# Linear attention and two expert MLPs on one core: a state tile without zero blocks, one masking per unit, other PSUM tiles and another start for the first sums of x

## The chip, the cores and the metric

The kernel runs on one core of a Trainium2 chip. The metric is the device time of one execution in microseconds; less is better. The kernel before takes 1306.77 us (median of three runs, 1305.92 to 1308.89).

The core has five engines with a queue each: PE (TensorE, matrix products into PSUM), DVE (VectorE), ACT (ScalarE), POOL (GpSimd) and SP (SyncE, which issues most DMAs). An engine runs its queue in order and waits on semaphores for the others.

## The reference

Three stages, cut to what is computed:

```python
# attention: state per batch and head, one step per token
state = alpha[:, :, t, :, None] * state + einsum('bhd,bhde->...', k[:, :, t], v[:, :, t])
y[:, :, t] = einsum('bhd,bhde->bhe', q[:, :, t], state)      # B=4, H=8, S=768, D=48
x = y as [3072, 384]
# first MLP
h = x @ w_in                                                  # 384 -> 2048
x = elu(h) @ w_out                                            # 2048 -> 384
# second: four experts, weighted by normalised probabilities
out = sum over e of p[:, e:e+1] * (relu(x @ w1[e]) @ w2[e])   # 384 -> 1024 -> 384
```

## The kernel before

**Attention** runs in chunks of 128 tokens: 6 chunks x 4 batches make 24 units. Heads lie in pairs, one at partitions 0 to 47, the other at 64 to 111. A unit has these steps (`unit_steps`, L333):

- `prep0` to `prep2` (L174 to L208): running products P of alpha (a scan on DVE), 1/P by logarithm and exponential on ACT, then k/P and q*P on DVE.
- `scores` (L210): eight matmuls of 48 rows, keys times queries, into two one-bank tiles (one for each j); DVE multiplies each by the causal mask (L224) into sm.
- `ktrans` (L230): four transposes of the keys into a third bank; ACT copies them to kn.
- `yout_t` (L257): four matmuls of the old state against the queries (L265; the stationary side is 112 columns wide: two heads of 48 with 16 unused columns between, zeros off the diagonal) and eight of values against masked scores (L272) into one bank; ACT copies the sum to yt (L277) and sends it to memory, from where SP loads it back as xr in the layout of the MLP. Units of the first chunk use `yout` instead.
- `state` (L287): eight matmuls of keys by values (L295), then DVE adds the old state and multiplies by P of the last token, once for each half of the partitions (L306, L308).
- `xtrans` (L312): high and low parts of the result in fp32r for the MLP.

The functions `abank` and `hbank` take PSUM banks in turn. Outside the warm-up the attention's banks are a0 and a1; the MLP's are h0 to h2, and t0 to t2 hold its result.

**First MLP.** 96 items: 6 blocks of 512 tokens, 16 slices of the hidden width each. `first(i)` is nine matmuls of 128 x 512 (L370: three parts of the width, each as high x high, high x low and low x high) and the elu: relu and exp on ACT (L381, L382), one DVE operation (L383), and the split of g into high (ACT, L330) and low (DVE, L331). `second(i-2)` is nine matmuls into t0 to t2 (L393). After a block's last item ACT copies t0 to t2 to x1raw (L850) and sends it out. The steps of a block's four units are spread over the items of the previous block. Here a list scheduler sets the order of the instructions on each engine from the order in which the code issues them; in the warm-up (the first chunk's units) and in the expert part the order on PE is the order of the code.

**First pair's sums.** `prep_x0` (L499) loads parts of the MLP's result, forms sums of them on POOL into the tile xs (L497), and splits these in fp32r: ACT rounds (L330), POOL subtracts (L331). xs lies in W1, a buffer that holds two slices of the MLP's weights until the last block has used them.

**Expert part.** 3 rounds of two chunks, 11 groups each. `layer1` makes 15 products of three matmuls (L650) into h banks, which DVE and POOL combine (L664, L666, L670), then relu on ACT and the low part on POOL (L628 to L630). `layer2` (L678) accumulates into six banks (m, d); the last matmul of an expert for (m, d) is followed by `gate` (L709): DVE multiplies the bank by the probabilities (L716, L719). Its matmuls of group i - 1 are dealt among the products of group i. In group 0 the last two `second()` stand there instead.

## Time and profile before

| what | us |
|---|---|
| median of three runs | 1306.77 |
| the profiled execution | 1309.81 |
| its span | 1308.1 |
| PE busy | 1258.4 (96%) |
| DVE busy | 890.6 (68%) |
| ACT busy | 582.7 (45%) |
| POOL busy | 518.4 (40%) |

The span runs from the first to the last instruction of the profiled execution; the execution's own time is 1.7 us longer. Busy time adds up the durations of an engine's instructions. PE is the only engine near the whole span. Of the chain of work that ended last, 65% of the span lies on PE, 11% each on DMA and DVE, 5% each on ACT and POOL. The mean granted clock of PE is 0.986 of full speed.

### The profile page before, as it was taken

How to read it: one execution, taken by the hardware profiler on the slowest of the kernel's cores; microseconds unless marked ns; L12 is line 12 of the kernel's file. 1: busy time of each engine (PE TensorE's matmuls, PEld its weight loads, DVE VectorE, ACT ScalarE, POOL GpSimd, SP SyncE). 2: the span in 40 equal slices, each digit the busy share in tenths (PEclk: the TensorE clock that was granted, in tenths of full speed). 3: DMA queues.
4: the chain of work that ended last, by engine and by line, in shares of the span. 5: the costliest groups of instructions: out<-in, count | busy, mean ns of one | idle time of the engine just before them, and what ended most of it. 6: DMA issues, size and time to landing. Idle time of an engine off the chain costs nothing.

```text
span 1308.1 us, 17463 instructions
## 1 busy us (share of the span) xinstructions
PE 1258.4 (96%) x6297; PEld 1014.6 (78%) x6297; DVE 890.6 (68%) x1546; ACT 582.7 (45%) x1076; POOL 518.4 (40%) x405
## 2 busy tenths in 40 slices
PE   8989999999999998889999999899999999999997
PEld 5676788778778787668888888788888878888886
DVE  9999988687777742366757666566667575767664
ACT  5666666566556564433434241333333233333241
POOL 0000000000000015348878474887966465447472
PEclk9999999999999999999999999999999999999999
DMA  6545366556666541425747348765645574525232
GB/s 246 195 164 178 109 221 239 189 203 214 242 223 216 188 147 73 173 93 194 258 159 278 114 161 335 256 243 183 255 167 199 185 296 166 195 97 204 102 109 75
DMA packets 71533, 246.67 MB, mean 189 GB/s; under 512 B 6680, under 2 KB 38264, under 8 KB 62096
## 3 DMA queue, kind: packets, MB, share of 16 engines
q1 hardware_dynamic: 68016, 236.84, 50.5%
q10 hardware_dynamic: 3424, 8.65, 1.9%
q8 instruction: 51, 0.84, 0.3%
q14 instruction: 42, 0.34, 0.1%
HBM read 182.11 MB, written 63.36 MB: 188 GB/s over the span
## 4 chain that ended last, share of the span: by engine, by line
PE 65%; DMA 11%; DVE 11%; ACT 5%; POOL 5%; issue 2%; SPq 1%; ACTq 0%; DVEq 0%; POOLq 0%
PE h L650 22%; PE t L700 13%; PE a L700 9%; PE t L393 7%; PE h L370 7%; DMA wraw<-in_we_dram 5%; PE h L700 4%; DMA x0d<-yt 2%; DMA raw<-in_att_dram 2%; DVE u L670 1%; DMA xr<-x0d 1%; DVE wh L331 1%; DVE P L181 1%; POOL xs L497 1%; DVE h L383 1%
## 5 line engine op out<-in xcount | busy, mean ns | idle before, releaser
L670 DVE TENSOR_TENSOR u<-h,u 128x512 f32<-128x512 f32 x258 | 177.5, 688 | 90.4 <-PE h L650 89.4
L393 PE MATMUL t<-g,w_W 128*128 128x512 f32 x864 | 226.1, 404 | 13.1 <-ACT g L330 12.5
L370 PE MATMUL h<-x,w_W 128*128 128x512 f32 x864 | 224.0, 402 | 3.7 <-ACT w_W L330 3.7
L650 PE MATMUL h<-xc_Q,wa 128*128 128x512 f32 x780 | 219.9, 391 | 3.3 <-DVE g L331 1.4
L630 POOL TENSOR_TENSOR g_W<-c,g_W 128x512 fp32r<-128x512 f32 x128 | 164.8, 1303 | 123.6 <-ACT c L629 105.5
L393 PEld LDWEIGHTS t<-g,w_W 128*128 128x128 f32 x864 | 162.5, 192 | 53.0 <-ACT g L330 14.6
L628 ACT ACTIVATE g_W<-c 128x512 fp32r<-128x512 f32 x128 | 80.0, 626 | 274.5 <-DVE c L670 159.9
L370 PEld LDWEIGHTS h<-x,w_W 128*128 128x128 f32 x864 | 162.8, 192 | 42.5 <-ACT w_W L330 5.1
L331 POOL TENSOR_TENSOR xc_X<-xr,xc_X 128x512 fp32r<-128x512 f32 x2 | 2.6, 1300 | 478.9 <-DMA xr<-x1d 478.7
L650 PEld LDWEIGHTS h<-xc_Q,wa 128*128 128x128 f32 x780 | 145.4, 188 | 37.4 <-DVE u L670 3.8
L700 PE MATMUL t<-g_W,wb 128*128 128x512 f32 x576 | 157.6, 389 | 0.0
L700 PEld LDWEIGHTS t<-g_W,wb 128*128 128x128 f32 x576 | 108.0, 188 | 22.6 <-POOL g_W L630 0.2
L629 ACT ACTIVATE c<-c 128x512 f32<-128x512 f32 x192 | 121.0, 632 | 7.4
L670 DVE TENSOR_TENSOR c<-u,h 128x512 f32<-128x512 f32 x123 | 84.1, 686 | 50.4 <-PE h L650 38.4
L664 DVE COPY u<-h 128x512 f32<-128x512 f32 x99 | 68.1, 690 | 68.3 <-PE h L650 68.0
L700 PE MATMUL a<-g_W,wb 128*128 128x512 f32 x384 | 112.0, 391 | 0.0
L630 POOL TENSOR_TENSOR g_X<-c,g_X 128x512 fp32r<-128x512 f32 x64 | 82.5, 1303 | 62.6 <-ACT c L629 52.0
L628 ACT ACTIVATE g_X<-c 128x512 fp32r<-128x512 f32 x64 | 40.0, 626 | 142.0 <-DVE c L670 78.5
L383 DVE SCALAR_TENSOR_TENSOR h<-e,h 128x512 f32<-128x512 f32 x96 | 66.5, 692 | 49.7 <-ACT e L382 49.2
L331 DVE TENSOR_TENSOR g<-h,g 128x512 fp32r<-128x512 f32 x96 | 66.0, 687 | 37.7 <-ACT g L330 36.7
L650 PE MATMUL h<-xc_W,wa 128*128 128x512 f32 x297 | 85.0, 395 | 4.9 <-DVE u L670 2.9
L700 PEld LDWEIGHTS a<-g_W,wb 128*128 128x128 f32 x384 | 72.4, 188 | 15.4 <-POOL g_W L630 0.3
(150 smaller groups left out, 1965.1 us busy)
## 6 DMA issues: line engine op xcount, KB each, us to landing
wa<-wad SPq DMA_DIRECT2D x33, 1536.0 KB, 6.6
wb<-wbd SPq DMA_DIRECT2D x30, 1536.0 KB, 6.5
raw<-in_att_dram SPq DMA_DIRECT2D x22, 960.0 KB, 5.1
wad<-wh SPq DMA_DIRECT2D x44, 384.0 KB, 2.8
wbd<-wh SPq DMA_DIRECT2D x43, 384.0 KB, 3.4
xcd<-xh SPq DMA_DIRECT2D x30, 512.0 KB, 3.7
wraw<-in_wm_dram SPq DMA_DIRECT2D x16, 768.0 KB, 4.3
wraw<-in_we_dram SPq DMA_DIRECT2D x20, 576.0 KB, 5.3
```

The costliest lines, as they stand in the source:

```text
L181: nc.vector.tensor_tensor_scan(P[:, a, :], raw[:, A0 + a * C:A0 + (a + 1) * C], self.plo.to_broadcast([128, C]), 1.0, ALU.mult, ALU.max,)
L331: (eng or nc.vector).tensor_tensor(out=lo, in0=src, in1=hi.bitcast(F32), op=ALU.subtract)
L370: nc.tensor.matmul(h[:, 0:n], w[:, wl, fi, k * 128:(k + 1) * 128], x[:, xl, k, n0:n0 + n], start=(k == 0 and i == 0), stop=(k == KD - 1 an ...
L383: nc.vector.scalar_tensor_tensor(out=h, in0=e, scalar=-1.0, in1=h, op0=ALU.add, op1=ALU.max)
L393: nc.tensor.matmul(self.xa[k][:, 0:n], w[:, wl, fi, DM + k * 128:DM + (k + 1) * 128], g[:, gl, 0:n], start=(f == 0 and i == 0), stop=(f == ...
L628: nc.scalar.activation(out=g[:, n, 0], in_=v, func=AF.Relu)
L629: nc.scalar.activation(out=v, in_=v, func=AF.Relu)
L630: nc.gpsimd.tensor_tensor(out=g[:, n, 1], in0=v, in1=g[:, n, 0].bitcast(F32), op=ALU.subtract)
L650: nc.tensor.matmul(b, w[:, wl], x[:, xl], start=(j == 0), stop=(j == 2))
L664: nc.vector.tensor_copy(out, b)
L670: (nc.vector if "b" in (a0, a1) or dst == "S5" else nc.gpsimd).tensor_tensor(out=out, in0=val(a0, b), in1=val(a1, b), op=ALU.add if op == ...
L700: nc.tensor.matmul(oa[m, d], wt[:, f, wl, d * 128:(d + 1) * 128], G[m][:, f, gl], start=first, stop=last)
```

## The change

- The state tile is 64 columns wide and without the zero blocks. The four matmuls of state against queries become eight of 48 rows and 64 columns (L271); the stationary side of `state`'s matmuls is 64 columns wide; DVE updates the state with one add and one multiplication over all 128 partitions.
- The eight score matmuls write one tile "a" of two banks, and one DVE operation masks all 1024 columns.
- `ktrans` follows the scores directly and takes an h bank. `state` follows `yout_t` directly in the order of the code, and `prep1` and `prep2` stand by themselves around the two.
- `yout_t` takes a new tile "a" and writes its first half; `state` writes the second half of the same tile (`abank`). In the warm-up the banks t0 to t2 serve.
- `layer2` accumulates m = 0 in the two halves of such a tile and h2, and m = 1 in t0 to t2.
- `prep_x0` begins at item b5 - 1 in place of b5 + 5 and spreads its 20 steps over 14 items in place of 9; xs lies in X0 (the MLP's input of the blocks with even number) in place of W1; the tiles xc and wa take other buffers accordingly, and xc tiles are taken as they are needed.
- The h banks stay three during group 0 of the expert part.

Lines after L114 shift by up to 6: L265 becomes L271, L272 L278, L277 L283, L295 L301, L330 L331, L650 L652, L700 L703, L716 L719, L719 L722, L850 L853. L370, L381 to L383 and L393 keep their numbers.

PE around one unit's state and output, kernel before (second chunk's first units; x is the MLP's input, sm the masked scores, st the state, kn the transposed keys):

```order
L235 MATMUL a_1597<-ident,raw 128x128 [waits DVE_49]
L235 MATMUL a_1597<-ident,raw 128x128 x3
L370 MATMUL h_1612<-x_1_689,w_W_640 128x512 x9
L265 MATMUL a_1629<-raw,st_150 112x128 [waits DVE_49]
L265 MATMUL a_1629<-raw,st_150 112x128 x3
L272 MATMUL a_1629<-sm,raw 48x128 x8
L393 MATMUL t_1504<-g,w_W_532 128x512 [waits Activation_49]
L393 MATMUL t_1504<-g,w_W_532 128x512 x2
L393 MATMUL t_1505<-g,w_W_532 128x512 x3
L393 MATMUL t_1506<-g,w_W_532 128x512 x3
L295 MATMUL a_1661<-raw,kn 48x48 [waits Activation_49]
L295 MATMUL a_1661<-raw,kn 48x48 x7
```

The same steps of a unit in the changed kernel, from the first() ahead of the state's product on:

```order
L370 MATMUL h_2445<-x_0_1490,w_W_636 128x512 [waits DVE_49]
L370 MATMUL h_2445<-x_0_1490,w_W_636 128x512 x8
L271 MATMUL a<-raw,st_150 64x128 [waits DVE_49]
L271 MATMUL a<-raw,st_150 64x128 x7
L278 MATMUL a<-sm,raw 48x128 x8
L393 MATMUL t_2309<-g,w_W_516 128x512 [waits Activation_49]
L393 MATMUL t_2309<-g,w_W_516 128x512 x2
L393 MATMUL t_2310<-g,w_W_516 128x512 x3
L301 MATMUL a<-raw,kn 64x48 [waits Activation_49]
L301 MATMUL a<-raw,kn 64x48 x7
L393 MATMUL t_2311<-g,w_W_516 128x512 x3
L370 MATMUL h_2512<-x_0_1490,w_W_734 128x512 [waits PE_49]
```

The transposes (L235) have gone up to the scores; the state's matmuls (now L301) stand six wide matmuls (L393) behind yout_t's last one (L278) where nine stood, write the same tile, and wait for ACT.

PE at the end of the first expert for the accumulators that come last, kernel before (t_5391 to t_5393 are t0 to t2):

```order
L700 MATMUL t_5391<-g_W_5749,wb 128x512 [waits Activation_49]
L700 MATMUL t_5391<-g_W_5749,wb 128x512 [waits Pool_49]
L700 MATMUL t_5391<-g_W_5749,wb 128x512
L650 MATMUL h_5863<-xc_Q_4864,wa 128x512 [waits DVE_49]
L650 MATMUL h_5863<-xc_Q_4864,wa 128x512 x2
L700 MATMUL t_5392<-g_W_5749,wb 128x512 x3
L650 MATMUL h_5878<-xc_Q_4864,wa 128x512 [waits DVE_49]
L650 MATMUL h_5878<-xc_Q_4864,wa 128x512 x2
L700 MATMUL t_5393<-g_W_5749,wb 128x512 x3
L700 MATMUL t_5391<-g_W_5749,wb 128x512
```

The same place in the changed kernel (a is the tile of two banks):

```order
L703 MATMUL a<-g_W_5704,wb 128x512
L652 MATMUL h_5845<-xc_Q_4933,wa 128x512 [waits DVE_49]
L652 MATMUL h_5845<-xc_Q_4933,wa 128x512 x2
L703 MATMUL a<-g_W_5704,wb 128x512 x2
L703 MATMUL a<-g_W_5704,wb 128x512 [waits DVE_49]
L652 MATMUL h_5860<-xc_W_5017,wa 128x512 x3
L703 MATMUL a<-g_W_5704,wb 128x512 x2
L703 MATMUL h_5351<-g_W_5704,wb 128x512
L652 MATMUL h_5869<-xc_W_5017,wa 128x512 x3
L703 MATMUL h_5351<-g_W_5704,wb 128x512 x2
```

Where the step from the first to the second accumulator stood without a wait (t_5391 to t_5392), the first matmul into the second half of a waits for DVE.

ACT at the end of the fifth block, kernel before (h_4643 and h_4686 are the last block's first two items, x1raw the copies of the fifth block's result):

```order
L381 ACTIVATE e<-h_4643 128x512 [waits PE_49]
L382 ACTIVATE e<-e 128x512 [waits Activation_49]
L330 CAST g<-h_4643 128x512 [waits DVE_49]
L381 ACTIVATE e<-h_4686 128x512 [waits PE_49]
L382 ACTIVATE e<-e 128x512 [waits Activation_49]
L850 COPY x1raw<-t_4033 128x512 [waits PE_49]
L850 COPY x1raw<-t_4034 128x512 [waits PE_49]
L330 CAST g<-h_4686 128x512 [waits DVE_49]
L850 COPY x1raw<-t_4035 128x512 [waits PE_49]
L851 DMA x1d_70<-x1raw 128x1536 [waits DMAHW1_49,Activation_49]
```

The same place in the changed kernel (h_4600 and h_4662 are the last block's first two items):

```order
L381 ACTIVATE e<-h_4600 128x512 [waits PE_49]
L331 CAST xc_Q_4776<-xs 128x512 [waits Pool_49]
L382 ACTIVATE e<-e 128x512 [waits Activation_49]
L331 CAST xc_Q_4776<-xs 128x512 [waits Pool_49]
L331 CAST xc_Q_4933<-xs 128x512 [waits Pool_49]
L331 CAST g<-h_4600 128x512 [waits DVE_49]
L331 CAST xc_Q_4933<-xs 128x512 [waits Pool_49]
L381 ACTIVATE e<-h_4662 128x512 [waits PE_49]
L853 COPY x1raw<-t_3986 128x512 [waits PE_49]
L382 ACTIVATE e<-e 128x512 [waits Activation_49]
L853 COPY x1raw<-t_3987 128x512 [waits PE_49]
L853 COPY x1raw<-t_3988 128x512 [waits PE_49]
```

The roundings of the sums xs, which all stood behind these copies, now stand in part ahead of them.

The diff, without the parts that only follow from it:

```diff
@@ -112,9 +112,14 @@
-    def abank(self):
-        self.an += 1
-        return self.bank(self.ab[self.an % len(self.ab)])
+    def abank(self, new=False):
+
+        if self.ab:
+            self.an += 1
+            return self.bank(self.ab[self.an % len(self.ab)])
+        if new:
+            self.a2 = self.ps.tile([128, 2, 512], F32, tag="a", name="a")
+        return self.a2[:, 0 if new else 1]
@@ -135,7 +140,7 @@
         for b in range(B):
-            s = self.ap.tile([128, NP, SW], F32, tag=f"st{b}", name=f"st{b}")
+            s = self.ap.tile([128, NP, 64], F32, tag=f"st{b}", name=f"st{b}")
             nc.vector.memset(s, 0.0)
@@ -211,26 +216,25 @@
         raw = self.raw[u]
-        ps = [self.abank(), self.abank()]
+        ps = self.ps.tile([128, 2, 512], F32, tag="a", name="a")
         for a in range(NP):
                 nc.tensor.matmul(
-                    ps[j][:, a * C:(a + 1) * C], raw[r, K0 + a * C:K0 + (a + 1) * C],
+                    ps[:, j, a * C:(a + 1) * C], raw[r, K0 + a * C:K0 + (a + 1) * C],
                     raw[r, Q0 + a * C:Q0 + (a + 1) * C], start=True, stop=True,
                 )
-        for j in range(2):
-            sm = self.ap.tile([128, NP, C], F32, tag="sm", name="sm", bufs=2)
-            nc.vector.tensor_tensor(
-                out=sm, in0=ps[j].rearrange("p (a t) -> p a t", a=NP),
-                in1=self.mask.unsqueeze(1).to_broadcast([128, NP, C]), op=ALU.mult,
-            )
-            self.sm[u, j] = sm
+        sm = self.ap.tile([128, 2 * NP, C], F32, tag="sm", name="sm")
+        nc.vector.tensor_tensor(
+            out=sm, in0=ps.rearrange("p j (a t) -> p (j a) t", a=NP),
+            in1=self.mask.unsqueeze(1).to_broadcast([128, 2 * NP, C]), op=ALU.mult,
+        )
+        self.sm[u] = sm
         raw = self.raw[u]
-        ps = self.abank()
+        ps = self.hbank()
         for a in range(NP):
@@ -260,18 +264,20 @@
         raw = self.raw[u]
-        ps = self.abank()
+        ps = self.abank(True)
         for a in range(NP):
-            nc.tensor.matmul(
-                ps[0:SW, a * C:(a + 1) * C], self.st[b][:, a, :], raw[:, Q0 + a * C:Q0 + (a + 1) * C],
-                start=(a == 0), stop=False, skip_group_check=True,
-            )
+            for j in range(2):
+                r = slice(64 * j, 64 * j + D)
+                nc.tensor.matmul(
+                    ps[64 * j:64 * j + 64, a * C:(a + 1) * C], self.st[b][r, a, :], raw[r, Q0 + a * C:Q0 + (a + 1) * C],
+                    start=(a == 0), stop=False, skip_group_check=True,
+                )
         for a in range(NP):
                     ps[64 * j:64 * j + D, a * C:(a + 1) * C], raw[:, V0 + h * D:V0 + (h + 1) * D],
-                    self.sm[u, j][:, a, :], start=False, stop=True, skip_group_check=True,
+                    self.sm[u][:, j * NP + a, :], start=False, stop=True, skip_group_check=True,
                 )
@@ -282,32 +288,27 @@
         self.y[u] = x
-        del self.sm[u, 0], self.sm[u, 1]
+        del self.sm[u]
         raw, kn, pc = self.raw.pop(u), self.kn.pop(u), self.P.pop(u)[:, :, C - 1:C]
-        st = self.st[b]
+        st = self.st[b][:, :, 0:D]
         ps = self.abank().rearrange("p (a e) -> p a e", a=NP)
             nc.tensor.matmul(
-                ps[64 * j:64 * j + D, h // 2, 0:D],
-                kn[:, (h // 2) * C + 64 * j:(h // 2) * C + 64 * j + D],
+                ps[64 * j:64 * j + 64, h // 2, 0:D],
+                kn[:, (h // 2) * C + 64 * j:(h // 2) * C + 64 * j + 64],
                 raw[:, V0 + h * D:V0 + (h + 1) * D], start=True, stop=True, skip_group_check=True,
             )
+        src = ps[:, :, 0:D]
         if c:
             tmp = self.ap.tile([128, NP, D], F32, tag="tmp", name="tmp")
-        for j in range(2):
-            r, e = slice(64 * j, 64 * j + D), slice(64 * j, 64 * j + D)
-            src = ps[r, :, 0:D]
-            if c:
-                nc.vector.tensor_tensor(out=tmp[r], in0=src, in1=st[r, :, e], op=ALU.add)
-                src = tmp[r]
-            nc.vector.tensor_tensor(
-                out=st[r, :, e], in0=src, in1=pc[r].to_broadcast([D, NP, D]), op=ALU.mult
-            )
+            nc.vector.tensor_tensor(out=tmp, in0=src, in1=st, op=ALU.add)
+            src = tmp
+        nc.vector.tensor_tensor(out=st, in0=src, in1=pc.to_broadcast([128, NP, D]), op=ALU.mult)
@@ -333,12 +334,11 @@
         N = lambda f, *a: [] if nxt is None else [(f, (nxt,) + a)]
-        s = [[(self.scores, (u,))]]
+        s = [[(self.scores, (u,))] + ([] if last else [(self.ktrans, (u,))])]
         s.append(N(self.prep0))
-        s.append([] if last else [(self.ktrans, (u,))])
-        s.append([(self.yout_t, (u,))] + N(self.prep1))
-        s.append([] if last else [(self.state, (u,))])
-        s[-1] += N(self.prep2)
+        s.append(N(self.prep1))
+        s.append([(self.yout_t, (u,))] + ([] if last else [(self.state, (u,))]))
+        s.append(N(self.prep2))
         s.append([(self.xtrans, (u,))])
@@ -500,8 +500,7 @@
         x, s = {}, {}
-        tiles = [self.xc_tile() for _ in range(5)]
-        at = {p: (tiles[i // 3], i % 3) for i, p in enumerate(ORDER)}
+        tiles = []
@@ -512,7 +511,7 @@
-        tmp = self.big.tile([128, 6, 512], F32, tag="W1", name="xs")
+        tmp = self.big.tile([128, 6, 512], F32, tag="X0", name="xs")
         sn, v = [0], {}
@@ -526,7 +525,10 @@
         def one(p):
-            t, i = at[p]
+            i = ORDER.index(p)
+            if i % 3 == 0:
+                tiles.append(self.xc_tile())
+            t, i = tiles[i // 3], i % 3
             y = s[p] if p in s else v[p] if p in v else x[XSUM[p][0]]
@@ -585,7 +587,7 @@
     def xc_tag(self):
-        return ("Q0", "Q1", "Q2", "X0", "W0", "W5")[self.xn % 6]
+        return ("Q0", "Q1", "Q2", "W0", "W1", "W5")[self.xn % 6]
@@ -598,7 +600,7 @@
     def load_wa(self, i):
-        t = self.big.tile([128, 12, 2, 128], F32R, tag=("W2", "W1")[i % 2], name="wa")
+        t = self.big.tile([128, 12, 2, 128], F32R, tag=("W2", "X0")[i % 2], name="wa")
         self.nc.sync.dma_start(out=t.bitcast(F32), in_=self.wad[i % NG])
@@ -685,9 +687,10 @@
         if q == 0:
-            self.oa[r] = {
-                (m, d): self.bank((("t0", "t1", "t2"), ("a0", "a1", "h2"))[m][d]) for m in range(2) for d in range(KD)
-            }
+            a = self.ps.tile([128, 2, 512], F32, tag="a", name="a")
+            l1 = [self.bank(t) for t in ("t0", "t1", "t2")]
+            self.oa[r] = {(0, 0): a[:, 0], (0, 1): a[:, 1], (0, 2): self.bank("h2")}
+            self.oa[r].update({(1, d): l1[d] for d in range(KD)})
         oa = self.oa[r]
@@ -792,7 +795,7 @@
                 nf += 1
-        self.ab = ("a0", "a1")
+        self.ab = None
         pe_order.__exit__(None, None, None)
@@ -832,9 +835,9 @@
             for n, s in enumerate(self.prep_x0()):
-                at(b5 + 6 + n * 9 // 20, do, s)
-
-        at(b5 + 5, begin_x0)
+                at(b5 + n * 14 // 20, do, s)
+
+        at(b5 - 1, begin_x0)
         gs = {}
@@ -872,12 +875,13 @@
         pe_order.__enter__()
-        self.hb = ("h0", "h1")
         ng = NPR * NG
             work, first_work = [], {}
+            if i:
+                self.hb = ("h0", "h1")
             if i == 0:
...
```

## Rows read from the trace of the kernel before

**Rows 1.** Stretches: length, busy us (instructions) of PE, PEld, DVE, ACT, POOL, clock, DMA.
```profile
0.00:50.00 50.00, 43.90 (x341) 31.63 (x341) 44.60 (x90) 28.16 (x53) 1.09 (x8) 0.93 0.64 230
140.00:480.00 340.00, 330.96 (x2012) 266.08 (x2011) 259.71 (x568) 209.10 (x445) 0.00 (x0) 0.99 0.60 208
558.97:579.34 20.37, 17.33 (x67) 11.83 (x67) 13.93 (x22) 6.59 (x12) 6.00 (x5) 1.00 0.26 99
600.00:1308.00 708.00, 694.94 (x3043) 570.47 (x3041) 453.29 (x679) 237.31 (x394) 458.51 (x351) 1.00 0.54 195
```

**Rows 2.** PE's waits: total us, times, longest.
```profile
PE t L393 <- ACT g L330: 12.5, 4, 4.6
PE a L235 <- DVE sm L224: 8.3, 5, 2.8
```

**Rows 3.** Page part 5: busy us, mean ns; idle before.
```profile
L700 PE MATMUL t<-g_W,wb 128*128 128x512 f32 x576 | 157.6, 389 | 0.0
```

**Rows 4.** DVE groups of 0:150 by form, columns as before.
```profile
L331 DVE TENSOR_TENSOR w_W<-cv,w_W 128x768 fp32r<-128x768 f32 x16 | 15.3, 955 | 4.3 <-ACT w_W L330 4.3
...
L224 DVE TENSOR_TENSOR sm<-a,mask 128x512 f32<-128x512 f32 x14 | 9.4, 683 | 0.2 <-PE a L218 0.2
...
L306 DVE TENSOR_TENSOR tmp<-a,st 48x192 f32<-48x192 f32 x8 | 2.8, 352 | 0.1
```

**Rows 5.** Timeline, two units: start us, us, instruction (PE, ACT).
```profile
167.29 1.04 PE L265 MATMUL a<-raw,st 128*112 128x128 f32 x8
168.26 1.08 PE L272 MATMUL a<-sm,raw 128*48 128x128 f32 x16
169.27 2.34 PE L393 MATMUL t<-g,w_W 128*128 128x512 f32 x9
...
169.65 0.57 ACT L277 COPY yt<-a 112x512 f32<-112x512 f32 x1
...
363.11 1.08 PE L272 MATMUL a<-sm,raw 128*48 128x128 f32 x16
...
367.90 0.58 ACT L277 COPY yt<-a 112x512 f32<-112x512 f32 x1
```

**Rows 6.** Timeline, end of the MLP: POOL, then PE.
```profile
480.45 1.30 POOL L331 TENSOR_TENSOR xc_X<-xr,xc_X 128x512 fp32r<-128x512 f32 x1 [478.73 <-DMA xr<-x1d]
...
505.83 2.55 POOL L497 TENSOR_TENSOR xs<-xr 128x512 f32<-128x512 f32 x2 [19.56 <-PE t L393]
508.34 1.29 POOL L497 TENSOR_TENSOR xs<-xs,xr 128x512 f32<-128x512 f32 x1
...
511.71 2.20 PE L393 MATMUL t<-g,w_W 128*128 128x512 f32 x9
513.75 2.20 PE L370 MATMUL h<-x,w_W 128*128 128x512 f32 x9
...
519.52 0.50 PE L393 MATMUL t<-g,w_W 128*128 128x512 f32 x1 [3.58 <-ACT g L330]
520.25 3.68 PE L393 MATMUL t<-g,w_W 128*128 128x512 f32 x8 [0.23 <-DVE g L331]
...
530.61 4.04 PE L393 MATMUL t<-g,w_W 128*128 128x512 f32 x9 [4.61 <-ACT g L330]
534.49 1.75 PE L370 MATMUL h<-x,w_W 128*128 128x512 f32 x7
```

**Rows 7.** Timeline of PE, start of the expert part.
```profile
560.52 1.65 PE L650 MATMUL h<-xc_Q,wa 128*128 128x512 f32 x6 [1.39 <-DVE g L331]
```

**Rows 8.** Timeline, two expert ends: PE and DVE.
```profile
636.78 0.84 PE L700 MATMUL t<-g_W,wb 128*128 128x512 f32 x3
...
637.59 0.68 DVE L716 TENSOR_TENSOR acc<-t,pb 128x512 f32<-128x512 f32 x1
...
697.32 0.87 PE L700 MATMUL t<-g_W,wb 128*128 128x512 f32 x3
...
698.55 0.68 DVE L719 TENSOR_TENSOR c<-t,pb 128x512 f32<-128x512 f32 x1
```

More of the change, by code (lines that the diff above doesn't have):

```diff
@@ L248, in yout @@
             nc.tensor.matmul(
-                ps[:, h * D:(h + 1) * D], self.sm[u, h % 2][:, h // 2, :],
+                ps[:, h * D:(h + 1) * D], self.sm[u][:, (h % 2) * NP + h // 2, :],
                 raw[:, V0 + h * D:V0 + (h + 1) * D], start=True, stop=True, skip_group_check=True,
@@ L284, in yout_t @@
         self.y[u] = x
-        del self.sm[u, 0], self.sm[u, 1]
+        del self.sm[u]
     def state(self, u):
@@ L774, in run @@
         nf = 0
-        self.ab = ("a0", "a1", "t0", "t1", "t2")
+        self.ab = ("t0", "t1", "t2")
         for i in range(B + 1):
```

## The prediction, made before the changed kernel ran

> **What bounds the kernel now.** I read the busy shares by stretch first. From 600 us to the end PE is busy 694.9 of 708 us, DVE 453.3 [rows 1]: two thirds of the time is bound by PE alone, and whatever PE waits there is lost. From 140 to 480 PE is busy 331.0 of 340, so PE bounds that too. Only in the first 140 us does DVE lead: in the first 50 us it is busy 44.6, PE 43.9 [rows 1]. So I read PE's own waits next. Two stand out: the second matmuls of the MLP waiting for the rounded activation g, 12.5 us in 4 pieces, and the key transposes waiting for the masks, 8.3 us in 5 [rows 2]. The second-layer matmuls of the expert part (L700) stand with 0.0 us of idle time before them [rows 3]; the change has to be judged against that zero.
>
> **First 140 us.** DVE loses work there. An element-wise operation takes 0.955 us for 768 columns and 0.683 for 512 [rows 4], so 0.27 for 256 more, and about 1.22 for one mask of 1024 columns against 2 x 0.683: 0.15 saved per unit, 1.3 for the nine units that are masked in the first 150 us. The state's 24 operations in that time (8 of L306, 16 of L308) of 0.35 us on 48 rows [rows 4] become 12 on 128 rows; the spare rows cost nothing, since time follows columns; 4.2 saved. Together 5.5 us of an engine that is busy nine tenths. I take 3, because DVE also waits there and the order is dealt anew; bounds -6 and +4.
>
> **140 to 480 us: one wait goes, one comes.** The key transposes (L235, now L239) leave the banks that the mask reads and go into an h bank: the 8.3 us vanish. What is late next is yout_t, which needs the masked scores; it stands 27 wide matmuls behind the scores, about 6.1 us, and the one mask ends 0.55 us later than the first of two did, so I leave 1.5 us: -6.8. Running scores and transposes together takes away one return to wide matmuls per unit, up to 0.14 us (below): -1.
>
> Against that, the state's matmuls (L301) now write the second half of the tile whose first half the copy yt on ACT reads. The tile is one object, so PE waits for that copy, and the row in the order above shows it. A wide matmul starts every 2.04 / 9 = 0.227 us (511.71 to 513.75 [rows 6]). State's matmuls stand 4 to 6 of these behind yout_t's last one in most units (0.9 to 1.4 us) and 10 or 11 in the others. How long does the copy take to be done? In one unit yout_t ends at 168.26 + 1.08 = 169.34 and the copy at 169.65 + 0.57 = 170.22, 0.88 later; in another 364.19 and 368.48, 4.29 later, because casts of the weight preparation stand ahead of it on ACT [rows 5]. In the kernel before nobody on PE asks for this copy. Taking the lags of before for the nine units of the third to fifth chunk (batches 1 to 3) against 0.9 or 1.4 gives 8.8 us. The order on ACT in the changed kernel is milder in some: I take +7, bounds 2 and 13. Behind the waiting matmul stand the rest of that second() and the next first(), so nothing on PE covers it. "Two groups for four" is then really three, since wide matmuls still lie between yout_t and state.
>
> yout_t's four matmuls of 112 columns take 168.26 - 167.29 = 0.97 us. They become eight of 48 rows and 64 columns. Eight of L272, which also come in pairs on different parts of the array, take 169.27 - 168.26 = 1.01 [rows 5]. I take the new eight at the same, so nothing; the upper bound is eight at 0.24 one after the other, 0.97 more per unit, 15.5 us for the 16 units behind the first 140 us. The nine wide matmuls behind small ones last 2.34 us in place of 2.20 [rows 5, 6]; the new form can add such a step once or twice per unit, so I put +1.5 here, bounds 0 and 4.
>
> The Trainium skill ("TensorEngine Tiling (Array Packing)", Key Properties) says that different tiles can load weights and multiply in parallel, and that a change of the tiling mode drains the engine. The 1.01 us for eight agree with the first half and the 2.34 with the second; by the second alone the 64x64 form is one mode more in each unit, and the sum would go up by 20 x 0.14 = 2.8 us as an estimate.
>
> The stretch sums to -6.8 - 1 + 7 + 1.5 = about +1.
>
> **The stall near 520 us.** PE should run five wide groups from 511.71 in 10.2 us and needs 534.49 - 511.71 = 22.78: 12.6 us lost. 3.58, 0.23 and 4.61 are waits, and the rest is the half clock behind them (eight matmuls from 520.25 last 3.68 us, where nine last 2.20 at the full one) [rows 6]. The reason: POOL's sums of x start at 505.83, after 19.56 us of waiting for the W1 buffer, one every 1.25 us (505.83 to 508.34 for two) [rows 6], and ACT, which rounds them, stands blocked in its own order while PE needs g. The change gives the sums another buffer, X0, which comes free when the last first() of the fifth block ends; call this moment T0 (about 479). So POOL starts some 24 us earlier. But the roundings now stand earlier on ACT too: in the order above, three of them stand ahead of the relu of the last block's second item and of the three copies x1raw out of t0 to t2. The last of the three waits for POOL's 15th operation of this part. The first operations on the loads alone start at 480.45 [rows 6] and the sum needs later ones, so I put its start at T0 + 2.4; 15 x 1.25 = 18.8, so T0 + 21.2; rounding, relu and the first copy take some 0.6 each: T0 + 23.1. PE's second(80), which starts t0 anew, would come six groups after T0, at T0 + 12.2. So PE waits about 10.9 us, then pays the half clock once (1.8): 12.7 against 12.6. I count 0, bounds -4 and +4: the stall moves from 516-534 to about 491-504.
>
> **Start of the expert part.** Three h banks for two in the first of the 33 groups. That group takes 20.4 us [rows 1] for 4.1 us of second() and 15 products of 0.68, 14.3 in all, and 1.39 us go on a wait at 560.52 [rows 7]. DVE is busy 13.9 of the 20.4. I take -2.5, bounds 0 and -5.
>
> **The 708 us behind it.** Layer 2's accumulators for m = 0 are now the two halves of one tile. At each expert's end for m = 0 the last matmul into the first half is followed by the gate on DVE, which reads that half; the next matmul, into the second half, must wait for it. Before, the next matmul went to its own tile and ran on. It happens 4 x 3 = 12 times. The price from rows: in one place the three matmuls start at 636.78, the next would start 0.68 later at 637.46, the gate runs 637.59 to 638.27 with DVE free: 0.85 lost with the signal back. In another the three start at 697.32, the gate 698.55 to 699.23 because DVE's queue was ahead: 1.25 [rows 8]. Six of the twelve have one other DVE operation ahead (about 1.1), three have two (1.25), two more than that (1.9), the last none (0.9): 15 us. Bounds: only the gate itself, 12 x 0.68 = 8, and two operations ahead each time, 12 x 2.06 = 25. Queued behind it on PE are the products of the next group, and DVE, ACT and POOL live from those; nothing hides it.
>
> **Sum.** -3 + 1 + 0 - 2.5 + 15 = +10.5. The profiled execution took 1309.81 us (span 1308.1, 1.7 around it), so 1320.3 in its terms; it stands 3.04 above the median of 1306.77, so the median should be **1317 us**. A change below 0.2% (2.6 us) could not be told from none.
>
> **Rivals.**
> *The stall really goes.* If the roundings come early enough that ACT reaches the x1raw copies by T0 + 12.2, for which POOL would have to have done 15 operations in about 8 us, the 12.6 vanish: 1317 - 12.6 = 1304, and with the gates at their lower bound 1297: not slower. For it: POOL is idle until 505.83 apart from four operations. Against it: 1.25 us each in a row [rows 6]. It decides from the moment that the last rounding ahead of the copies is done before T0 + 11.
> *The gates are nearly free.* If PE finds the gate done, or gets the time back from waits for h banks that it would have had anyway, the 15 shrink to 3: 1305. Against it: PE is 98% busy there, so there is little to get back [rows 1].
> *The small matmuls do not overlap.* Then 15.5 more: 1332, and the groups of yout_t last 1.9 us each. For it: no row of before shows 48 rows by 64 columns. Against it: the eight of L272.
>
> **How the numbers follow.** Forecast 0.65, the stall goes 0.14, gates nearly free 0.10, no overlap 0.11. The forecast's own range is 1306 to 1328, from the bounds of the terms taken half together. Eight in ten: 1302 to 1331, which leaves out the lower half of the first rival and the end of the third. Faster: 0.10 from the first rival, 0.06 from the second, 0.04 from the forecast's low end: 0.20. Same: 0.09. Slower: 0.71.
>
> **What would show it.** In PE's waits of the changed kernel: no wait of the transposes for a mask; a wait of L301 for the copy yt, 5 to 12 us in all; twelve waits of L703 for DVE's gates, about 1 us each; the waits of L393 for g or x1raw still near 10 us, but before 505. The groups of yout_t take about 1 us. The forecast is wrong if L703 does not wait for DVE, or if PE runs through from 485 to 535.

## The result and the profile after

The changed kernel takes 1324.01 us (median of four runs, 1320.82 to 1324.26) against 1306.69 before (four runs): 1.0124 times as long, 95% interval 1.0105 to 1.0144. It is slower, as forecast, by 17.3 us where 10.5 were forecast. The profiled execution has a span of 1322.5 us, 14.4 more than the profiled one of before.

PE's waits of the changed kernel over the whole span (total us, times, longest) answer to [rows 2]:

```profile
PE a L703 <- DVE c L722: 11.9, 9, 1.8
PE a L301 <- ACT yt L283: 10.7, 9, 3.1
PE t L393 <- ACT x1raw L853: 10.1, 1, 10.1
...
PE a L703 <- DVE acc L719: 2.8, 3, 0.9
...
PE t L393 <- ACT g L331: 1.6, 1, 1.6
```

The two waits of [rows 2] are nearly gone: no transpose waits for a mask, and L393 waits 1.6 us for g. In their place stand the three that the prediction named: twelve waits of the second layer for a gate (11.9 + 2.8 = 14.7 us), nine of the state's matmuls for the copy yt, and one of second(80) for x1raw. The second layer's rows had 0.0 us of idle time before them [rows 3], and 0.0 and 0.1 for the accumulators that are in the tile a now. For that tile they read, with the names of g's two buffers:

```profile
L703 PE MATMUL a<-g_W,wb 128*128 128x512 f32 x384 | 115.3, 392 | 9.4 <-DVE c L722 7.6
...
L703 PE MATMUL a<-g_X,wb 128*128 128x512 f32 x192 | 58.4, 394 | 5.2 <-DVE c L722 4.3 <-DVE acc L719 0.9
```

Where the 14.4 us of the two profiles lie, by points in PE's program (the moments at which the first, the 144th and the 576th matmul of L393, the first of L650 and the first of L700 start; us):

| stretch | before | after | difference |
|---|---|---|---|
| start to the first MLP matmul of L393 | 50.7 | 49.6 | -1.1 |
| from there to the end of block 1 | 97.4 | 90.0 | -7.4 |
| blocks 2 to 4 | 262.3 | 267.5 | +5.2 |
| from there to the first product | 150.1 | 147.8 | -2.3 |
| group 0 of the expert part | 18.9 | 17.9 | -1.0 |
| the rest | 728.7 | 749.7 | +21.0 |

The first 140 us in two windows, from the start to the end of block 1, before and after (columns as in [rows 1]). DVE's busy time falls by 5.6 us, and the clock is 0.99 in place of 0.93:

```profile
0.00:148.10 148.10, 132.42 (x835) 99.65 (x836) 135.12 (x241) 90.06 (x163) 1.09 (x8) 0.93 0.50 174
```

```profile
0.00:139.60 139.60, 128.80 (x864) 95.03 (x868) 129.50 (x221) 88.96 (x163) 1.09 (x8) 0.99 0.54 184
```

A unit's state and output after, on PE (start us, us, instruction, idle time before it and what ended it), answers to [rows 5]:

```profile
340.33 1.09 PE L271 MATMUL a<-raw,st 48*64 48x128 f32 x16
341.35 1.08 PE L278 MATMUL a<-sm,raw 128*48 128x128 f32 x16
342.36 1.66 PE L393 MATMUL t<-g,w_W 128*128 128x512 f32 x6
344.58 0.67 PE L301 MATMUL a<-raw,kn 128*64 128x48 f32 x16 [0.56 <-ACT yt L283]
```

The eight matmuls of 48 rows and 64 columns take 1.02 us (four of 112 columns took 0.97), so they overlap in pairs. Six wide matmuls later the state's matmuls wait for the copy.

The stall at the end of the MLP after, POOL, ACT and PE, answers to [rows 6]:

```profile
477.63 1.29 POOL L497 TENSOR_TENSOR xs<-xr 128x512 f32<-128x512 f32 x1 [475.90 <-DMA xr<-x1d]
```

```profile
496.25 0.62 ACT L331 CAST xc_Q<-xs 128x512 fp32r<-128x512 f32 x1 [6.22 <-POOL xs L497]
496.77 0.59 ACT L381 ACTIVATE e<-h 128x512 f32<-128x512 f32 x1
497.26 0.58 ACT L853 COPY x1raw<-t 128x512 f32<-128x512 f32 x1
```

```profile
485.55 2.20 PE L370 MATMUL h<-x,w_W 128*128 128x512 f32 x9
497.89 4.11 PE L393 MATMUL t<-g,w_W 128*128 128x512 f32 x9 [10.14 <-ACT x1raw L853]
501.84 2.25 PE L370 MATMUL h<-x,w_W 128*128 128x512 f32 x9
```

POOL's sums start 28 us earlier, at 477.63; the rounding that waits for POOL's 15th operation stands ahead of a relu and the copy of t0, and PE stands for 10.14 us until that copy is done. The group behind it runs at a mean granted clock of 0.51, so nearly all of it at the lower of the clock's two levels (1.2 of 2.4 GHz), called half clock here, and its nine matmuls take 4.11 us in place of 2.20:

```profile
497.89:501.84 3.95, 3.95 (x9) 3.14 (x10) 2.08 (x3) 3.15 (x7) 3.95 (x4) 0.51 0.42 174
```

Two wide groups need 4.1 us and got 501.84 - 485.55 = 16.3: 12.2 lost, against 12.6 before.

One expert end after, PE and DVE, answers to [rows 8]:

```profile
631.84 0.61 PE L703 MATMUL a<-g_W,wb 128*128 128x512 f32 x2
633.38 0.50 PE L703 MATMUL a<-g_W,wb 128*128 128x512 f32 x1 [0.93 <-DVE acc L719]
633.72 0.86 PE L652 MATMUL h<-xc_W,wa 128*128 128x512 f32 x3
```

```profile
632.04 0.69 DVE L672 TENSOR_TENSOR u<-h,u 128x512 f32<-128x512 f32 x1 [0.17 <-PE h L652]
632.64 0.68 DVE L719 TENSOR_TENSOR acc<-a,pb 128x512 f32<-128x512 f32 x1
```

The gate stands behind one other operation, ends at 633.32, and PE goes on at 633.38. Without it the matmul would have started at 631.84 + 2 x 0.227 = 632.29: 1.09 us. From the first gate of one expert end to that of the next, the eleven stretches of the changed kernel are 1.2 to 2.2 us longer than those of before, 17.7 in all.

### The profile page after: what moved, and what is told of

Its sections match the earlier page's. It is cut to its first block, busy times and chain, and to the rows that moved or that the text cites. A ratio compares the mean times of both kernels' runs of the same rounds, so it can differ in the third digit from the quotient of the medians.

```text
span 1322.5 us, 17720 instructions
## 1 busy us (share of the span) xinstructions
PE 1261.8 (95%) x6453; PEld 1013.2 (77%) x6457; DVE 876.5 (66%) x1486; ACT 581.5 (44%) x1076; POOL 517.9 (39%) x405
## 4 chain that ended last, share of the span: by engine, by line
PE 72%; DVE 11%; DMA 7%; ACT 5%; POOL 3%; issue 2%; SPq 1%; ACTq 0%; DVEq 0%; POOLq 0%
PE h L652 23%; PE t L703 14%; PE h L370 9%; PE t L393 9%; PE a L703 9%; PE h L703 4%; DMA wraw<-in_we_dram 2%; DVE u L672 2%; DMA xr<-x0d 2%; DMA x0d<-yt 1%; DVE c L722 1%; DMA raw<-in_att_dram 1%; DVE P L186 1%; DVE h L383 1%; DVE sm L228 1%
## 5 line engine op out<-in xcount | busy, mean ns | idle before, releaser
L393 PE MATMUL t<-g,w_W 128*128 128x512 f32 x864 | 222.8, 399 | 11.9 <-ACT x1raw L853 10.1
L652 PE MATMUL h<-xc_Q,wa 128*128 128x512 f32 x780 | 220.2, 392 | 3.6 <-DVE c L672 2.4
L370 PE MATMUL h<-x,w_W 128*128 128x512 f32 x864 | 220.1, 396 | 1.6 <-ACT w_W L331 1.4
L393 PEld LDWEIGHTS t<-g,w_W 128*128 128x128 f32 x864 | 161.9, 191 | 49.0 <-ACT x1raw L853 10.6
L497 POOL TENSOR_TENSOR xs<-xr 128x512 f32<-128x512 f32 x8 | 10.1, 1274 | 475.9 <-DMA xr<-x1d 475.9
L370 PEld LDWEIGHTS h<-x,w_W 128*128 128x128 f32 x864 | 160.4, 189 | 38.8 <-ACT w_W L331 2.7
L652 PEld LDWEIGHTS h<-xc_Q,wa 128*128 128x128 f32 x780 | 146.3, 188 | 36.6 <-DVE c L672 3.7
L703 PE MATMUL t<-g_W,wb 128*128 128x512 f32 x576 | 161.1, 392 | 0.4 <-POOL g_W L632 0.4
L703 PEld LDWEIGHTS t<-g_W,wb 128*128 128x128 f32 x576 | 109.0, 189 | 23.8 <-POOL g_W L632 0.8
L703 PE MATMUL a<-g_W,wb 128*128 128x512 f32 x384 | 115.3, 392 | 9.4 <-DVE c L722 7.6
L652 PE MATMUL h<-xc_W,wa 128*128 128x512 f32 x390 | 111.5, 395 | 2.9 <-DVE u L672 2.9
L383 DVE SCALAR_TENSOR_TENSOR h<-e,h 128x512 f32<-128x512 f32 x96 | 66.4, 691 | 61.7 <-ACT e L382 61.2
L703 PEld LDWEIGHTS a<-g_W,wb 128*128 128x128 f32 x384 | 71.8, 188 | 27.7 <-DVE c L722 10.1
L652 PEld LDWEIGHTS h<-xc_W,wa 128*128 128x128 f32 x390 | 74.4, 192 | 19.7 <-DVE u L672 4.2
```

The source lines that it names most:

```text
L370: nc.tensor.matmul(h[:, 0:n], w[:, wl, fi, k * 128:(k + 1) * 128], x[:, xl, k, n0:n0 + n], start=(k == 0 and i == 0), stop=(k == KD - 1 an ...
L383: nc.vector.scalar_tensor_tensor(out=h, in0=e, scalar=-1.0, in1=h, op0=ALU.add, op1=ALU.max)
L393: nc.tensor.matmul(self.xa[k][:, 0:n], w[:, wl, fi, DM + k * 128:DM + (k + 1) * 128], g[:, gl, 0:n], start=(f == 0 and i == 0), stop=(f == ...
L652: nc.tensor.matmul(b, w[:, wl], x[:, xl], start=(j == 0), stop=(j == 2))
L703: nc.tensor.matmul(oa[m, d], wt[:, f, wl, d * 128:(d + 1) * 128], G[m][:, f, gl], start=first, stop=last)
```

## The experiments

All are measured against the kernel before in the same session; the sessions' medians of before are 1309.8 to 1311.8 us, so ratios are to be compared and not microseconds. The changed kernel itself was not measured again in these sessions.

**1. The gates' halves apart.** The changed kernel with the accumulators dealt differently:

```diff
-            self.oa[r] = {(0, 0): a[:, 0], (0, 1): a[:, 1], (0, 2): self.bank("h2")}
-            self.oa[r].update({(1, d): l1[d] for d in range(KD)})
+            self.oa[r] = {(0, 0): a[:, 0], (0, 1): l1[0], (0, 2): self.bank("h2")}
+            self.oa[r].update({(1, 0): a[:, 1], (1, 1): l1[1], (1, 2): l1[2]})
```

> The changed kernel, but layer 2 puts (0,0) and (1,0) into the two halves of the tile a, (0,1) into t0, (1,1) and (1,2) into t1 and t2: the two halves are then never written within nine matmuls of the other's gate. Theory (the wait for the gate that reads the other half of the same tile): PE's twelve waits of 14.7 us go; the twelve stretches from gate to gate, 1.2 to 2.2 us longer in the changed kernel than before, come back to their old length, so 18 to 20 us less: about 1305. Rival (DVE is late there for another reason, the order of the gates on it or the half clock, and PE would wait elsewhere): PE's waits stay in sum, 1320 to 1324.

Measured: 1303.72 us, 0.9944 of before (0.9925 to 0.9964), where the changed kernel has 1.0124. The kernels of experiments 2 to 4, measured in the same session with the gates as changed, take 1322.1 to 1325.4 us. No wait of L703 for DVE is left. From 600 us on PE waits for this alone:

```profile
PE h L652 <- DVE u L672: 5.1, 6, 2.9
PE h L652 <- DVE c L672: 2.2, 3, 1.0
PE a L703 <- POOL g_W L632: 0.6, 1, 0.6
```

The stretch from the first second-layer matmul to the end takes 732.7 us, against 749.7 and 728.7. Theory right: 17 of the 21 us, of which 1.7 are not the gates' but a piece of half clock that this run did not have (experiment 4). The other 4 lie in the first, second and fourth of the eleven stretches from gate to gate, which are 0.7, 1.7 and 1.5 us longer than before. In the first two PE waits 2.1 us for operations of DVE and POOL, before 0.2; in the fourth the mean granted clock is 0.95 for 0.98. The new deal of the banks is not shown to cost this: the 1.7 us turn up in the sixth stretch in place of the second both in experiment 8, which has the new deal, and in experiment 9, which has that of before.

**2. The state's matmuls ahead of the copy.** `state` is split; its matmuls go into `yout_t`, in front of the copy:

```diff
+        upd = None if c == NCH - 1 else self.state_mm(u)
         y = self.ap.tile([128, NP * C], F32, tag="y", name="yt")
         nc.scalar.copy(y[0:SW], ps[0:SW])
...
+        if upd is not None:
+            self.state_upd(u, upd)
```

> The changed kernel, but the state's matmuls are issued ahead of the copy yt in the code, so that they need not wait for it; they then stand directly behind those of yout_t on PE. Theory (PE waits in state for ACT's reading of the other half): the 10.7 us of nine waits go, and one return from small to wide matmuls per unit with them (some 0.14 x 16): 11 to 13 us less, about 1312. Rival (the wait moves: the next scores need both readers of the tile to be done, or the copy kn comes too late for the state's matmuls): less than half of it, 1318 to 1324.

Measured: 1324.82 us, 1.0108 (1.0076 to 1.0140): no gain. The state's matmuls now stand directly behind L278 and wait for nothing; but from 145 to 470 us PE waits elsewhere (lines of the split kernel: L382 is first(), L405 second(), L344 the split of g):

```profile
PE h L382 <- DVE g L344: 7.3, 7, 1.7
PE t L405 <- DVE g L344: 1.6, 4, 0.5
PE a L271 <- DVE sm L228: 0.7, 3, 0.4
PE t L405 <- ACT g L343: 0.5, 1, 0.5
```

10.1 us in place of 10.7. A first() does not read g; it waits for DVE to have read the h bank that it is to write. All seven waits of L382 are at the first or second first() behind a unit's transposes, which took one of the three h banks, as here:

```profile
241.93 1.16 PE L223 MATMUL a<-raw 48*128 48x128 f32 x16
243.03 0.66 PE L239 MATMUL h<-ident,raw 128*128 128x128 f32 x4
245.35 2.34 PE L382 MATMUL h<-x,w_W 128*128 128x512 f32 x9 [1.67 <-DVE g L344]
```

The rival was right that the wait moves, though it moved neither to the scores nor to kn, where the rival looked for it. The changed kernel's wait for yt covered the shortage of banks that ktrans brought.

**3. The sums as before.** The changed kernel with `prep_x0` begun at b5 + 5 over nine items, xs in W1, xc and wa as before.

> The changed kernel, but the first pair's sums start as in the kernel before (item b5 + 5, nine items, xs in W1, the buffers xc and wa as there). Theory (the stall is only moved by the change, 12.6 us at 520 before and about 12.3 at 488 to 502 after): no difference, 1322 to 1326, and PE's waits for g near 520 are back. Rival (the early start is worth something that the stall hides, such as free engines near the end of the MLP): slower by 3 or more. Other rival (it costs): faster by 3 or more.

Measured: 1322.14 us, 1.0093 (1.0065 to 1.0122), against 1.0124 (1.0105 to 1.0144) with the new start: no difference that the intervals allow to be told. The wait for x1raw is gone and the one for g is back:

```profile
PE t L393 <- ACT g L331: 10.3, 3, 5.0
```

**4. Two h banks in group 0.**

```diff
-            if i:
-                self.hb = ("h0", "h1")
+            self.hb = ("h0", "h1")
```

> The changed kernel, but group 0 of the expert part has two h banks. Theory (three banks save 2.6 us in that group, 17.8 against 20.4, and the wait of 2.2 us at its end with the half clock behind it gives about 2 back): 0 to 2 us slower. Rival (the third bank is worth its 2.6 in full): 2.6 slower. Other rival (the half clock behind the long wait costs more than the bank saves): 1 to 3 us faster.

Measured: 1325.38 us, 1.0101 (1.0071 to 1.0131); too close to 1.0124 to tell. The traces tell more. Group 0 from its first product, and then up to the small matmul of `flag`, in the changed kernel:

```profile
554.93:572.74 17.81, 15.58 (x67) 12.15 (x66) 13.60 (x22) 7.73 (x14) 7.17 (x6) 1.00 0.34 124
572.74:581.07 8.33, 8.33 (x31) 6.43 (x30) 4.16 (x7) 2.37 (x4) 8.17 (x7) 0.80 0.04 18
```

and with two banks:

```profile
557.90:577.53 19.63, 17.27 (x68) 11.59 (x66) 13.84 (x22) 6.57 (x12) 5.99 (x5) 1.00 0.27 98
577.53:584.20 6.67, 6.67 (x30) 5.26 (x28) 4.16 (x7) 2.91 (x5) 6.59 (x6) 1.00 0.16 66
```

The third bank saves 1.8 us in the group. With three, PE runs ahead and then waits 2.16 us for a bank; behind that wait the clock is 0.80 for 8.33 us, and the same work takes 1.7 us longer. In this execution nothing is left, as the theory said. But the wait alone does not bring the clock down. Experiment 1 has three banks and the same wait, 2.17 us, and these two stretches:

```profile
553.14:570.94 17.80, 15.55 (x68) 12.16 (x66) 13.60 (x22) 7.72 (x14) 7.16 (x6) 1.00 0.33 125
570.94:577.62 6.68, 6.68 (x31) 5.26 (x30) 4.17 (x7) 2.38 (x4) 6.60 (x6) 1.00 0.05 20
```

Experiments 2 and 5 (6.69 and 6.70 us) are like it, experiment 8 is like the changed kernel (0.80, 8.20 us), and experiment 3 lies between (0.85, 7.82 us). So the saving stands in some executions and is lost in others; what decides is not known.

**5. Gates apart, sums on DVE.** Experiment 1, and the two calls `self.sum_x(nc.gpsimd, ...)` of `prep_x0` with `nc.vector`.

> The changed kernel with the gates' halves apart (as in the first experiment, 0.994 of before) and, besides, the first pair's sums on DVE in place of POOL; POOL keeps the low parts. Theory (PE stalls 10.3 us and then pays the half clock because POOL's 1.25 us operations, sums and low parts in one row, hold ACT up, and ACT the copies x1raw): the sums are done on DVE in 0.7 us each, ACT reaches the copies some 11 us earlier, and the stall shrinks to 0 to 2 us: 10 to 12 us less than the first experiment, about 1292, 0.985 to 0.987 of before. Rival (ACT's own 15 roundings, or the loads, are what is late): less than half of it, 0.990 or more.

Measured: 1298.43 us, 0.9912 (0.9889 to 0.9935). The stall shrinks from 10.3 to 4.2 us, not to 0 to 2: the direction is right, the size is not. DVE's sums are slow there, and so is POOL beside them:

```profile
474.61 1.78 DVE L497 TENSOR_TENSOR xs<-xs,xr 128x512 f32<-128x512 f32 x1
476.31 1.77 DVE L497 TENSOR_TENSOR xs<-xs 128x512 f32<-128x512 f32 x1
```

```profile
472.38 3.46 POOL L332 TENSOR_TENSOR xc_Q<-xs,xc_Q 128x512 fp32r<-128x512 f32 x2
475.80 1.74 POOL L332 TENSOR_TENSOR xc_Q<-xr,xc_Q 128x512 fp32r<-128x512 f32 x1
```

**6. Experiment 2, transposes out of the h ring.** They stand behind prep0 and use the half of a new tile a that the state's matmuls write later.

```diff
-        ps = self.hbank()
+        ps = self.hbank() if self.ab else self.kbank()
...
+    def kbank(self):
+        self.abank(True)
+        return self.a2[:, 1]
```

> The second experiment's kernel (state's matmuls ahead of the copy yt), but the key transposes no longer take an h bank: they stand later, behind prep0, in the half of the tile a that the state's matmuls write afterwards. Theory (the seven waits of 7.3 us for the low part of g, all at one of the two first() behind the transposes, come from the h bank that the transposes take out of the ring of three): these waits fall to under 1 us, and in their place the transposes wait for the mask, 2 to 8 us in all, as in the kernel before; time 1318 to 1325. Rival (the elu on ACT and DVE is late for its own reasons, and the bank doesn't matter): the waits for g stay at 5 us or more.

Measured: 1333.37 us, 1.0177 (1.0153 to 1.0202). No wait of first() for the low part of g is left, which agrees with the bank as the cause; it does not prove it, since PE now stands 17.5 us at other places, and that would give the banks time to come free as well. The time was forecast 10 us too low. From 145 to 470 us (L243 are the transposes, L275 yout_t):

```profile
PE a L243 <- DVE sm L232: 14.6, 7, 3.5
PE a L275 <- ACT kn L247: 2.9, 3, 1.3
```

14.6 us where 2 to 8 were expected and 8.3 stood before [rows 2]: at all seven waits eighteen wide matmuls, about 4.4 us, lie between scores and transposes, one mask of 1.2 us ends later than two of 0.7 that are waited for one by one, and other operations stand ahead of it in DVE's queue.

**7. All together**: 1, 5, 2 and 6.

> All of it together: the gates' halves apart, the sums on DVE, the state's matmuls ahead of the copy yt, the transposes in a. Theory: the parts lie in different stretches and add up; with the sums at -11 and the gates at -20 from the changed kernel and the last two at 0 to -4: 1288 to 1293. Rival (time gained in the attention's stretch is given back at the end of the MLP, where the sums wait for the loads): no better than gates and sums alone.

Measured: 1309.37 us, 1.0004 (0.9984 to 1.0025), 11 us more than experiment 5. A miss: part 6 brings its loss (14.8 us of waits for the mask), which I had counted as 0 to -4. That the parts add up is not shown either: part 6 raises the ratio by 0.0053 from the changed kernel's and by 0.0092 here.

**8. Gates apart, sums and low parts on DVE.** Experiment 5, and in `one`:

```diff
-            self.split(t[:, i, 0], t[:, i, 1], y, nc.gpsimd)
+            self.split(t[:, i, 0], t[:, i, 1], y)
```

> The changed kernel with the gates' halves apart, and both the first pair's sums and their low parts on DVE; POOL does nothing there. Theory (in the fifth experiment the stall shrank from 10.3 only to 4.2 us because DVE's sums took 1.2 to 1.8 us in place of 0.7 while POOL worked on the low parts beside them): alone, DVE's operations on two operands in SBUF take 0.7 us each, the copies x1raw come in time, and the stall and the half clock behind it go: 0 to 1 us of wait, 4 to 7 us less than the fifth experiment's 0.9912, about 0.986 to 0.988. Rival (the operations of x sums are slow on DVE by themselves, by their layout): they stay above 1.1 us, with 27 of them DVE is busy for 30 us, the g of the last block comes late, and the time is no better than the fifth experiment's.

Measured: 1291.13 us, 0.9860 (0.9838 to 0.9881): the fastest kernel here, 1.4% below the kernel before. With POOL idle the same operations take 0.69 us, and PE runs through (DVE, then PE):

```profile
478.02 0.69 DVE L497 TENSOR_TENSOR xs<-xs 128x512 f32<-128x512 f32 x1
478.62 0.69 DVE L497 TENSOR_TENSOR xs<-xs,xr 128x512 f32<-128x512 f32 x1
```

```profile
480.80 2.20 PE L393 MATMUL t<-g,w_W 128*128 128x512 f32 x9
482.84 2.20 PE L370 MATMUL h<-x,w_W 128*128 128x512 f32 x9
484.88 2.20 PE L393 MATMUL t<-g,w_W 128*128 128x512 f32 x9
486.92 2.20 PE L370 MATMUL h<-x,w_W 128*128 128x512 f32 x9
```

**9. The kernel before with the new state alone.** L271's form for L265's, 64-column kn, one add and one multiplication.

> The kernel before, with one part of the change alone: the state without zero blocks (eight matmuls of 48 rows x 64 columns for four of 112 columns, one add and one multiplication on 128 partitions for two of each). Theory (in the first 140 us DVE's work counts in full; behind that each 64-column form costs PE 0.1 to 0.2 us per unit): DVE's busy time to the end of the first block falls by 4.2 us and so does the end of that block, 148.1 before; from there to the fifth block's end 1 to 3 us longer; together 0 to 3 us less, 0.998 to 1.000. Rival (the first stretch of the changed kernel is shorter because of the order of its steps, not of DVE's work): the end of the first block moves by less than 2 us.

Measured: 1318.91 us, 1.0058 (1.0037 to 1.0080): slower, where no change or a little less was expected. By the test as it was written the rival holds: the end of block 1 moves from 148.1 to 146.5 us, less than 2. From the first matmul of L393 to that end it takes 92.5 us against 97.4, but the mean granted clock there is 0.98 for 0.93, so this gain is not shown to be DVE's. And that matmul starts at 54.0 us for 50.7, with a clock of 0.87 for 0.93 up to it; among these kernels it starts at 49.5 and 49.6 in the two with 0.97 there, and at 52.4 and 54.0 in the two with 0.87. Blocks 2 to 4 take 270.8 us for 262.3: PE is busy 259.8 for 253.9 and waits 11.0 for masks, not 8.3. The wider stationary side explains part of the busy time: the state's eight matmuls take 0.60 us for 0.50, and L271's eight 0.06 more than L265's four, 0.16 x 12 units = 1.9 us. The clock in that stretch is 0.981 for 0.993; as an estimate from these means, the time at half clock costs 270.8 x 0.019 - 262.3 x 0.007 = 3.3 us more.

## Why the prediction was right, and where its sizes were off

- **The gates** (+15): right in mechanism, place and number of waits. The waits are 14.7 us as idle time, but that leaves out that PE starts up again: the matmul at 633.38 could have started 1.09 us earlier, not 0.93, and the next comes 0.34 us behind it, not 0.23. From start to start the twelve delays are 1.0 to 2.0 us and 16.6 in all, where 0.9 to 1.9 and 15 were forecast; the slow matmul behind each adds 0.11, 1.3 in all, for which the forecast had no term. The eleven stretches grew by 17.7 us; behind the two longest waits, 1.8 us each, there is more half clock than before (last section).
- **The wait for yt** (+7): right. It was 10.7 in the changed kernel's profile and 6.5, 9.1, 7.8, 4.4 and 7.9 in the five others with the same attention code (experiments 1, 3, 4, 5, 8); mean 7.7. Blocks 2 to 4 less this wait take 255.0 to 256.8 in all six, 254.0 before less its own wait of 8.3: PE's own work grew by 1 to 3 us, where +0.5 (small matmuls less merging) was forecast: by 1.0 to 1.8 in the three with a mean granted clock of 0.993 or 0.994 in this stretch (0.993 before), by 2.3 to 2.8 in the three with 0.987. With the wait, the stretch takes 263.8 on average over the six, 1.5 more than before; the +5.2 of the changed kernel's profile holds the longest of these waits.
- What was wrong in this step is its meaning. I wrote that nothing on PE covers this wait. Experiment 2 shows that it covers another: take it away, and first() waits for its h bank. The prediction counted ktrans's move into the h banks as a gain of 6.8 with no price, and did not ask who else needs them.
- **The first 140 us** (-3, bound -6): mis-sized; 8.5 us were gained. DVE's work fell by 5.6, as worked out (5.5). That it counted in full is not shown, because the clock rose with it: from the first L393 to the end of block 1 its mean is 0.93 before and 1.00 after, and as an estimate from these means the half clock there cost 97.4 x 0.07 = 6.8 us before and nothing after. The gain in this part was 7.4 us. In the five others with this attention code it was 5.3 to 8.0, with clocks of 0.98 to 1.00. In experiments 2 and 6 DVE's work to the end of block 1 fell as much (to 129.6 and 129.9 us), the clock was 0.95, and the part became 2.3 us shorter and 0.5 us longer. The forecast had no term for the clock.
- **The stall** (0): right, by its own steps: PE stood 10.1 us (10.9 forecast) at 488 to 498 (491 to 504 forecast), for the copy of t0, behind the rounding that waits for POOL's 15th operation. Experiment 3 puts the whole edit at nothing that the intervals can tell, experiment 8 shows what the stall was worth: 0.9944 to 0.9860.
- **Group 0** (-2.5): right in size. The forecast's 20.4 us begin with the wait of 1.39 us ahead of the first product [rows 7]; the changed kernel has no such wait and takes 17.8, so 2.6 are saved, of which the table above has 1.0 in group 0 and the rest in the line before it. The forecast left out what is late next, the wait of 2.16 us, and the half clock behind it took 1.7 back in this execution, though not in experiments 1, 2 and 5.
- **No overlap of small matmuls** (rival): ruled out by 1.02 us for eight. The Trainium skill ("TensorEngine Tiling (Array Packing)", Key Properties) says that different tiles can multiply in parallel, and the trace agrees.

The sum, forecast against the two profiles: -3 against -8.5 up to the end of block 1, +1 against +5.2 in blocks 2 to 4, 0 against -2.3 from there to the first product, -2.5 against -1.0 in group 0, +15 against +21.0 behind it (17.7 from gate to gate, 1.7 of half clock behind group 0, 1.6 at the last end). That is 14.4 for 10.5. That the two come so near is partly luck: two terms came out 5.5 and 2.3 us below the forecast, three 4.2, 1.5 and 6.0 above it. The medians differ by 17.3 because the profiled execution of before stands 3.1 above its median and that of after 0.3 above its own.

## What to carry to other kernels

A tile of two banks was one object for the order of the work here: whoever wrote one half waited for whoever read the other (L703 for the gates, L301 for the copy yt). Put into it only what is written together and read together, or what is far apart in time; another deal of the same six banks was worth 1.8% by the ratios of experiment 1, and 18.8 us, 1.4%, between the two profiled executions. Before taking a wait away, look at what stands ready behind it, and which ring of buffers the cure draws on.

## What the runs showed of the hardware that I had not expected

DVE's operation on two operands in SBUF takes 0.69 us for 128 x 512 when POOL is idle (experiment 8) and 1.19 to 1.78 when POOL runs such operations beside it (experiment 5), and POOL's go from 1.25 to 1.7 us. DVE's operations with one operand in PSUM kept their 0.68 to 0.70 us in the same stretch. The Trainium skill ("SBUF — State Buffer", SBUF: two separate sides) says that these two engines share a pair of ports and lock each other out, a DVE operation with two SBUF inputs against a POOL operation that reads SBUF; the traces agree. So moving work from POOL to DVE pays more when all of it moves.

How long PE had waited did not settle what its clock did next. Behind the wait of 2.15 to 2.17 us at the end of group 0 the mean granted clock was 0.80 for 8.3 us in the changed kernel (572.74 to 581.07) and for 8.2 us in experiment 8, but 1.00 in experiments 1, 2 and 5, where the same work took 6.7 us. In the expert part of the changed kernel, three stretches of 10 us have 0.83: two behind the gates' longest waits, 1.81 and 1.82 us (820 to 830, 1070 to 1080), one where a wait of 2.66 us for DVE's operations on the products ends (850 to 860). Behind the gates' waits of 0.9 to 1.3 us up to 1300 us the clock did not fall.
